# Loads ahead of the gate setup, eight output buffers, a short last slot and an earlier first unit in a block-sorted attention feeding a mixture of experts

## The chip, the core and the metric

The kernel runs on one core of a Trainium2 chip. The metric is the device time of one execution in microseconds (us). The core has a matrix engine (TensorE: PE in the profile, its weight loads PEld), a vector engine (VectorE, DVE), an activation engine (ScalarE, ACT), a general engine (GpSimd, POOL) and a sync engine (SyncE, SP). Each works off its own instructions in program order; they meet through semaphores. POOL and SP also issue the DMAs: POOL all bulk loads and all indirect scatters, SP the small loads and the transposing reads.

## What is computed

```python
# attention: batch 4, heads 8, seq 768, head_dim 64, 8 blocks of 96
P = sort_net                                  # (4, 8, 8, 8)
for _ in range(5):                            # Sinkhorn
    P = exp(P - max(P, -1)); P = P / sum(P, -1); P = P / sum(P, -2)
k_sorted = einsum('bhij,bhjcd->bhicd', P, k_blocks)
v_sorted = einsum('bhij,bhjcd->bhicd', P, v_blocks)
attn = softmax(q_blocks @ k_sorted.T / 8) @ v_sorted    # per block
x = attn as (3072 tokens, 512)
# mixture of experts: 8 experts, one per token, F = 1024
logits = x @ w_gate + modality_bias[modality_id]
e = argmax(logits); gate = softmax(logits)[e]
out[token] = gate * (relu(x[token] @ w1[e]) @ w2[e])
```

In the inputs drawn here two experts take all tokens, one 1559 rows and the other 1513.

## The kernel before

**Stages.** The two halves of the batch are groups g = 0 and 1. For each group `sort_k` multiplies the k blocks with the Sinkhorn matrix, `sort_v` does so for v (64 matmuls of 128 columns in all per group). Then the attention runs in 32 units u = 0 to 31 (16 a group): `scores(u)` writes PSUM, `expo(u)` takes the exponential on ACT, `av(u)` multiplies with v and normalises on DVE into `xb`. `spread_q` (called by `prep_s`, a DVE copy) and `prep_q` (PE transposes and one evacuation) make the queries of a unit. `scores(1)` stands behind `prep_q(2)` in PE's order, and that needs the spread made by `prep_s(2)`.

**Routing.** Eight units make a quarter m (0 to 3) of the tokens. `gate_T`/`gate_L` (lines 395 to 413) form the logits in four steps, `choose(m)` takes the argmax on DVE, `place(m)` (line 437) ranks the tokens on PE (`rk`, line 444) and scatters the rows to DRAM (`xs_scratch`) by eight indirect DMAs on POOL (line 472), sorted by expert. `table(m)` computes on DVE which slots of 256 rows are now full.

**Experts.** 13 slots of up to 256 rows. Slots 0 to 11 alternate between the two experts, slot 12 takes the leftover of one. A slot is fetched by `x_fetch` (transposing DMA on SP, line 584, plus a small one for row numbers and gates, line 587) and worked off in six pieces: four `mL1(s, j)` (8 matmuls of 256 columns each into `hp`, then a relu on DVE or ACT) and two `mL2(s, t)` (8 matmuls of 512 columns into `yp`, gate product into one of four `y` buffers, indirect DMA to `out`, line 638). Slot 12 reads its weights at an address from a register.

**Order.** `tc.manual_schedule()`: program order is each engine's order. The main loop over u issues `scores(u)`, `expo(u)`, the work listed in `A1[u]`, `p1` pieces, `av(u-1)`, `prep_q(u+2)`, `prep_s(u+3)`, the work listed in `A2[u]`, `p2` pieces. `pace(u)` gives p1 and p2. The sort of group 1 is spread over units 6 to 15 by `A2`. Which of ACT and DVE evacuates a PSUM tile is decided by `pick` when the program is built.

**Around the change.** Behind the sort of group 0 stand, in this order, `prep_q(0)`, `prep_q(1)`, a mask and an iota on POOL, `gate_consts()` (line 265: `perm_mult` multiplies on POOL into `ptmpw`, line 191, and reduces on DVE into `wgf`, line 192; then six small POOL operations), and only then the loads of k, v, weights (expert 0) and the first half of the queries for group 1. In POOL's order they come behind `gate_consts`. `load_w(1)` and the second half of the queries, `load_q(1, 1)`, are issued in `A2[9]`, right behind `place(0)`.

Of the kernel before, what the change touches and what calls it, by code (L numbers as in the profile page):

```python
# [17 lines left out]
def kernel(  # L18
# [28 lines left out]
    NS = 13  # L47
# [23 lines left out]
    k_raw = kvb[:, RW:2 * RW]  # L71
    v_cols = kvb[:, 0:128 * D].rearrange("p (c d) -> p d c", d=D)
# [7 lines left out]
    xTg = [singles.tile([128, 8, BLK], BF16, tag=f"xTg{z}", name=f"xTg{z}") for z in range(2)]  # L80
    y_b = [singles.tile([128, Dm], FP32, tag=f"y{z}", name=f"y{z}") for z in range(4)]
    xT_b = [singles.tile([128, 4, PR], BF16, tag=f"xT{z}", name=f"xT{z}") for z in range(3)]
    idg_b = [singles.tile([128, 2, 2], I32, tag=f"idg{z}", name=f"idg{z}") for z in range(4)]
    hT_b = [qTb[0][:, 2048 + z * 2048:4096 + z * 2048].rearrange("p (f r) -> p f r", f=8) for z in range(2)]
    zpad = singles.tile([128, GW], BF16, tag="zpad")
# [29 lines left out]
    def load_q(g, hh):  # L115
        t = q_in(g, hh).rearrange("p (r h f) -> p r h f", r=2, h=4)
        for par in range(2):
            nc.gpsimd.dma_start(out=t[:, par], in_=q[2 * g + par, 4 * hh:4 * hh + 4]
                                .rearrange("h (p t) d -> p h (t d)", t=6))

# [65 lines left out]
    def perm_mult(dst, srcs, nm):  # L186
        eng = nc.gpsimd if nm == "w" else nc.vector
        tmp = small.tile([128, 4, E, E], FP32, tag=f"ptmp{nm}", name=f"ptmp{nm}")
# [304 lines left out]
    def table(m):  # L493
# [29 lines left out]
        if last:  # L523
            mk, t1 = t_("mk", 2), t_("t1", 1)
            nc.vector.tensor_tensor(a, f[:, 0:2], d2, ALU.subtract)
            nc.vector.tensor_scalar(mk, a, 0.0, None, ALU.is_gt)
            nc.vector.tensor_tensor(t1, mk[:, 0:1], mk[:, 1:2], ALU.mult)
# [53 lines left out]

    def x_fetch(s, row, own, after=()):
        view = xs_dram[bass.ds(row, PR)]
        i1 = nc.sync.dma_start_transpose(out=xT_b[s % 3], in_=view.bitcast(BF16)[:, 0:Dm])
        if own:
            nc.sync.nop()
        i2 = nc.sync.dma_start(out=idg_b[s % 4], in_=pair_rows(row)[:, :, Dm // 2:GW // 2])
        if own:
            for i in (i1, i2):
                in_xs_group(i.ins, after)  # L590
                for a in after:
                    tc.add_manual_dep(i.ins, a.name, SYNC, reason="rows of the slot")

    def x_load(s, after=()):
# [5 lines left out]
        row = nc.values_load(tb[0:1, n:n + 1], engines=(SPEng,), min_val=0, max_val=ZR)  # L600
        x_fetch(s, row, True, after)

    evs = {}

    def mE(s):
        evs[s] = nc.values_load(tabL[0:1, 1:2], engines=(PEng,), min_val=0, max_val=WCOL)

    def w_at(s, off, n):
        if s in evs:
            return w01[:, bass.ds(evs[s] + off, n)]  # L610
        return w01[:, (s % 2) * WCOL + off:(s % 2) * WCOL + off + n]

    def mL1(s, j):
        hp = mipsum.tile([128, 2, PR], FP32, tag="mi", name=f"hp{s}_{j}")
        for f in range(2):
            for c in range(4):
                nc.tensor.matmul(hp[:, f], w_at(s, c * F + (2 * j + f) * 128, 128), xT_b[s % 3][:, c],  # L617
                                 start=(c == 0), stop=(c == 3))
        hd = hT_b[s % 2][:, 2 * j:2 * j + 2]
        if not pick(0.61, 0.7):  # L620
            nc.vector.tensor_scalar(hd, hp, 0.0, None, ALU.max)  # L621
        else:
            nc.scalar.activation(hd, hp, ACT.Relu)  # L623

    def mL2(s, t):
        yp = mipsum.tile([128, Dm], FP32, tag="mi", name=f"yp{s}_{t}")
        for fc in range(8):
            nc.tensor.matmul(yp, hT_b[s % 2][:, fc, t * 128:(t + 1) * 128],  # L628
                             w_at(s, 4 * F + fc * Dm, Dm), start=(fc == 0), stop=(fc == 7))
        idg = idg_b[s % 4]  # L630
        y = y_b[(2 * s + t) % 4]
        gate = idg.bitcast(FP32)[:, t, 1:2]
        if pick(0.7, 0.7):
            nc.scalar.activation(y, yp, ACT.Copy, scale=gate)  # L634
        else:
            nc.vector.tensor_scalar(y, yp, gate, None, ALU.mult)  # L636
# [5 lines left out]
        tc.add_to_no_dep_group("out", ins.ins)  # L642

# [5 lines left out]
    def late_consts():  # L649
# [28 lines left out]
    nc.gpsimd.iota(zpad.bitcast(I32)[:, Dm // 2:Dm // 2 + 1], pattern=[[0, 1]], base=SKIP, channel_multiplier=0)  # L678
# [62 lines left out]
    def run_pieces(n):
        for _ in range(n):
            if st["pos"] >= len(pieces):
                return
            for f, a in pieces[st["pos"]]:
                f(*a)
                if f is mL1 and a[1] == 3:
                    st["l1"] = a[0] + 1
                if f is mL2 and a[1] == 1:
                    st["done"] = a[0] + 1  # L750
                if f is not mE:
                    x_try()
            st["pos"] += 1

    def pace(u):
        if u < 16:
            return 0, 0
        if u < 22:
            return 1, 1
        if u < 24:  # L760
            return 0, 0
        if u < 30:
            return 1, 1
        return 1, 1

    prep_s(2)
    for u in range(32):
        p1, p2 = pace(u)
        scores(u)
        expo(u)  # L770
        for f, a in A1.get(u, []):
# [15 lines left out]
    choose(3)  # L787
    run_pieces(1)
    place(3)
# [35 lines left out]
    nc.vector.tensor_tensor(tR2, rv, sF256[:, 0:NREST], ALU.add)  # L825
    evs.clear()
    for s in range(NREST):
# [40 lines left out]
```

## Time and profile before

| | us |
|---|---|
| median of 3 runs | 257.69 (254.66 to 259.04) |
| the profiled execution | 253.83 |
| its span, first to last instruction | 252.1 |
| PE busy in it | 176.5 (70%) |
| DVE / ACT / POOL busy in it | 102.7 / 93.5 / 73.8 |

All rows of the trace belong to the profiled execution: times are us from the start of its span. In a timeline row stand start, duration, engine, line, operation, output tile <- input tiles, shapes, count, and in brackets the idle time of the engine before it with what ended it. PEclk is the granted clock of TensorE as a share of its full 2.4 GHz; 0.5 is 1.2 GHz.

### The profile page before, as it was taken

The numbers are of one execution on the slowest core, as the hardware profiler recorded it, in microseconds if no ns is written. First come the engines' busy times: TensorE is split into PE (matmuls) and PEld (weight loads), VectorE is DVE, ScalarE is ACT, GpSimd is POOL, SyncE is SP. The second block draws the span as 40 slices with busy tenths as digits, with TensorE's granted clock in tenths as the row PEclk, the third lists the DMA queues.
The fourth block names the chain that finished last, engine by engine and source line by source line (L and its number), as shares of the span: only waits on it lengthen the run. The fifth ranks groups of instructions, "written<-read, shape, count | busy, mean of one in ns | idle before, by whom it ended". The sixth has DMA issues, their size and how long they took to land.

```text
span 252.1 us, 5223 instructions
## 1 busy us (share of the span) xinstructions
PE 176.5 (70%) x2046; PEld 126.8 (50%) x2046; DVE 102.7 (41%) x340; ACT 93.5 (37%) x146; POOL 73.8 (29%) x101
## 2 busy tenths in 40 slices
PE   0079689785880968189869249998808999999800
PEld 0079578674770735065654136665603666665300
DVE  6858775862660561045463013435401233322200
ACT  2148667555580423154432224433203322232200
POOL 7201380035610027401106700322761223333110
PEclk9999965957586779569797858999986999999965
DMA  5999779999799902531102365231545343322000
GB/s 88 218 201 193 105 134 217 200 189 203 165 192 188 154 13 83 135 64 42 44 3 62 101 131 43 84 86 43 163 106 130 106 125 104 111 83 78 4 15 0
DMA packets 33840, 27.78 MB, mean 110 GB/s; under 512 B 22543, under 2 KB 29455, under 8 KB 33552
## 3 DMA queue, kind: packets, MB, share of 16 engines
q0 software_dynamic: 11840, 23.10, 41.7%
q1 hardware_dynamic: 21968, 4.28, 12.1%
q8 instruction: 18, 0.29, 0.5%
q14 instruction: 14, 0.11, 0.1%
HBM read 27.33 MB, written 10.78 MB: 151 GB/s over the span
## 4 chain that ended last, share of the span: by engine, by line
PE 21%; issue 19%; DMA 9%; POOL 8%; another core or an unknown queue 5%; DVE 4%; ACT 2%; POOLq 1%; DVEq 0%; ACTq 0%
PE yp L628 8%; DMA q_in<-in_q_dram 7%; PE hp L617 7%; POOL out_dram L638 6%; POOL xs_scratch L472 2%; PE sc L366 1%; DMA xs_scratch<-xb,dest 1%; PE lg L404 1%; PE gt L398 1%; DVE xb L389 1%; PE op L385 1%; ACT xTg L295 1%; ACT attnT L372 1%; POOLq L638 1%
## 5 line engine op out<-in xcount | busy, mean ns | idle before, releaser
L617 PE MATMUL hp<-xT,w 128*128 128x256 bf16 x416 | 57.8, 290 | 6.7 <-DMA xT<-xs_scratch 6.7
L628 PE MATMUL yp<-w,qT 128*128 128x512 bf16 (+1 forms) x208 | 52.8, 407 | 7.9 <-ACT qT L623 7.9
L617 PEld LDWEIGHTS <-w 128*128 128x128 bf16 (+1 forms) x416 | 41.4, 103 | 17.4 <-issue 7.3
L472 POOL DMA_INDIRECT xs_scratch<-xb,dest x32 | 29.4, 917 | 67.0 <-issue 63.2
L638 POOL DMA_INDIRECT out_dram<-y,idg x26 | 25.4, 976 | 77.1 <-ACT y L634 53.6
L628 PEld LDWEIGHTS <-qT 128*128 128x128 bf16 x208 | 20.7, 103 | 32.1 <-ACT qT L623 9.4
L623 ACT ACTIVATE qT<-hp 128x512 bf16<-128x512 f32 x33 | 19.6, 596 | 44.5 <-PE hp L617 33.5
L372 ACT ACTIVATE attnT<-sc 96x768 bf16<-96x768 f32 x32 | 25.8, 808 | 17.0 <-remote 9.4
L621 DVE TENSOR_SCALAR qT<-hp 128x512 bf16<-128x512 f32 x19 | 13.1, 692 | 44.8 <-PE hp L617 34.4
L634 ACT ACTIVATE y<-yp,idg 128x512 f32<-128x512 f32 x18 | 12.4, 687 | 35.9 <-PE yp L628 25.6
L389 DVE TENSOR_TENSOR xb<-op,rs 96x512 bf16<-96x512 f32 x32 | 22.0, 687 | 1.4 <-DMA q_in<-in_q_dram 0.2
L404 PE MATMUL lg<-wgp,xTg 128*96 128x8 bf16 x128 | 9.9, 201 | 17.7 <-ACT xTg L295 15.4
L388 DVE RECIPROCAL rs<-op 96x8 f32<-96x8 f32 x32 | 6.4, 199 | 35.4 <-PE op L385 20.3
L404 PEld LDWEIGHTS <-xTg 128*96 128x96 bf16 x128 | 8.9, 151 | 19.1 <-ACT xTg L295 15.9
L636 DVE TENSOR_SCALAR y<-yp,idg 128x512 f32<-128x512 f32 x8 | 6.0, 751 | 29.7 <-PE yp L628 27.0
L385 PE MATMUL op<-v_sb,attnT 96*128 96x65 bf16 x256 | 15.8, 211 | 0.2 <-issue 0.2
L295 ACT CAST v_sb<-va 96x512 bf16<-96x512 f32 (+1 forms) x23 | 13.3, 641 | 5.8 <-PE va L317 4.6
L385 PEld LDWEIGHTS <-attnT 96*128 96x128 bf16 x256 | 13.5, 110 | 3.2 <-issue 0.6
L308 PEld LDWEIGHTS <-kvb 128*64 128x64 bf16 x384 | 9.8, 145 | 9.5 <-issue 9.3
L295 ACT COPY qT<-tq 128x768 bf16<-128x768 bf16 x12 | 9.6, 799 | 12.4 <-PE tq L350 12.4
L366 PE MATMUL sc<-qT,kT 64*128 64x96 bf16 (+1 forms) x256 | 13.1, 232 | 1.5 <-ACT attnT L372 1.2
L317 PE MATMUL va<-bd,kvb 128*128 128x128 bf16 x128 | 13.7, 275 | 0.0
(155 smaller groups left out, 171.2 us busy)
## 6 DMA issues: line engine op xcount, KB each, us to landing
w<-in_moe_w_dram POOLq DMA_DIRECT2D x4, 1024.0 KB
kvb<-in_k_dram POOLq DMA_DIRECT2D x4, 768.0 KB
kvb<-in_v_dram POOLq DMA_DIRECT2D x2, 1536.0 KB
v_sb<-in_q_dram POOLq DMA_DIRECT2D x4, 384.0 KB
q_in<-in_q_dram POOLq DMA_DIRECT2D x4, 384.0 KB
xs_scratch<-zpad SPq DMA_DIRECT2D x3, 258.0 KB
xs_scratch<-xb,dest POOLq DMA_INDIRECT x32
out_dram<-y,idg POOLq DMA_INDIRECT x26
```

Of the source, the lines that this page charges most:

```text
L295: (nc.scalar.copy if pick(act, dve) else nc.vector.tensor_copy)(dst, src)
L317: nc.tensor.matmul(acc[:, z], v_cols[:, d0 + z], bd[g], start=True, stop=True)
L366: nc.tensor.matmul(sc[0:m, par, j * BLK:(j + 1) * BLK], kT[g][rows, x0:x0 + m], qT[rows, i], start=True, stop=True)
L372: nc.scalar.activation(attnT[u % 2][:, 0:8 * BLK].rearrange("p (r f) -> p r f", r=2), sc_tiles.pop(u)[0:BLK, :, 0:4 * BLK], ACT.Exp, scale ...
L385: nc.tensor.matmul(ov[:, par, j], attnT[u % 2][:, c0:c0 + 128], v_sb[g][0:BLK, par * 64 + h * 8 + i, 0:D + 1], start=True, stop=True)
L389: nc.vector.tensor_tensor(xt[:, :, h * D:(h + 1) * D].rearrange("p (r j) d -> p r j d", r=2), ov[0:BLK, :, :, 0:D], rs.broadcast_to([BLK, ...
L404: nc.tensor.matmul(lg[:, t], xTg[c % 2][:, t], wgp[:, c], start=True, stop=True)
L472: ins = nc.gpsimd.indirect_dma_start(out=xs_dram, out_offset=bass.IndirectOffsetOnAxis(ap=dest[:, t:t + 1], axis=0), in_=xt.bitcast(I32)[: ...
L617: nc.tensor.matmul(hp[:, f], w_at(s, c * F + (2 * j + f) * 128, 128), xT_b[s % 3][:, c], start=(c == 0), stop=(c == 3))
L623: nc.scalar.activation(hd, hp, ACT.Relu)
L628: nc.tensor.matmul(yp, hT_b[s % 2][:, fc, t * 128:(t + 1) * 128], w_at(s, 4 * F + fc * Dm, Dm), start=(fc == 0), stop=(fc == 7))
L638: ins = nc.gpsimd.indirect_dma_start(out=out, out_offset=bass.IndirectOffsetOnAxis(ap=idg[:, t, 0:1], axis=0), in_=y, in_offset=None, boun ...
```

## The change

1. k of group 1 gets a place of its own in `kvb` (a gap of 2048 columns is put in and zeroed by DVE at the start), and its two loads are issued after the k sort of group 0. The loads of v, of the first half of the queries and of the weights of expert 0 come before `gate_consts`, which now stands between `scores(0)`/`expo(0)` and `prep_q(1)`.
2. `prep_s(0)`, `prep_q(0)`, `scores(0)` and `expo(0)` are called inside the v sort (after jobs 13 and 16 of 21).
3. `load_q(1, 1)` and `load_w(1)` move from `A2[9]` to `A1[10]` and wait until the transposing read of slot 0 has landed.
4. `place(1)` and `place(2)` move one step later, behind the next unit's `scores`; `table_x` follows them. Two pieces instead of one between `choose(3)` and `place(3)`.
5. Eight `y` buffers in `kvb`, four `xT` and six `idg` buffers, `hT` 0 in a tile of its own.
6. From slot 6 on the `mL1` of the next slot are mixed with the `mL2` of the current one. Pieces run from u = 17 on, two a unit, without the pause at 22 and 23 (30 pieces in the loop instead of 28).
7. Slot 12 takes up to 128 rows: rows stationary, 512 columns of w1 moving (`last_L1`), eight transposes (`last_T`), one `last_L2`, the gate product split between ACT and DVE.

```diff
-    kvb = singles.tile([128, 2 * RW], BF16, tag="kvb")
+    KO = 128 * D
+    kvb = singles.tile([128, KO + RW], BF16, tag="kvb")
...
+    NY, NX, NI = 8, 4, 6
+    yo = [KO + z * 2 * Dm for z in range(6)] + [RW + z * 2 * Dm for z in range(2)]
+    y_b = [kvb[:, o:o + 2 * Dm].bitcast(FP32) for o in yo]
...
+    nc.vector.memset(kvb[:, RW:KO], 0.0)
...
+    def last_L1(n):
+        if n == 0:
+            lreg["w"] = nc.values_load(tabL[0:1, 1:2], engines=(PEng,), min_val=0, max_val=WCOL)
+        hp = mipsum.tile([128, 512], FP32, tag="mi", name=f"hl{n}")
+        for c in range(4):
+            nc.tensor.matmul(hp, xT_b[SL % NX][:, c, 0:128], wl_at(c * F + n * 512, 512),
+                             start=(c == 0), stop=(c == 3))
+        relu(hrow[n], hp)
+    def last_T():
...
+        for f in range(8):
+            nc.tensor.transpose(tp[:, f], hrow[f // 4][:, (f % 4) * 128:(f % 4 + 1) * 128], ident)
...
+    def last_L2():
...
+        for fc in range(8):
+            nc.tensor.matmul(yp, hT_b[SL % 2][:, fc, 0:128], wl_at(4 * F + fc * Dm, Dm),
+                             start=(fc == 0), stop=(fc == 7))
...
+    make_upper_triangular(nc, maskUT, val=1.0, diag=False)
...
     for n, (f, g, x0, kd) in enumerate(g0):
         f(g, x0, kd)
...
             late_consts()
-        if n == 17:
+            load_k(1, 0)
+            load_k(1, 1)
+        if n == 13:
             prep_s(0)
-    prep_q(0)
+        if n == 16:
+            prep_q(0)
+            scores(0)
+            expo(0)
+    load_v(1)
+    load_q(1, 0)
+    load_w(0)
+    gate_consts()
     prep_q(1)
-    make_upper_triangular(nc, maskUT, val=1.0, diag=False)
...
-    gate_consts()
-    load_k(1, 0)
-    load_k(1, 1)
-    load_v(1)
-    load_w(0)
-    load_q(1, 0)
     zero_block()
...
+    def late_loads():
+        first = load_q(1, 1)
+        tc.add_manual_dep(first.ins, xins[0].ins.name, SYNC, reason="rows of the first slot go ahead")
+        load_w(1)
...
-            at2(8 * m + 9, place, m)
-            at1(8 * m + 10, table_x, m)
-    at2(9, load_w, 1)
-    at2(9, load_q, 1, 1)
+            at2(8 * m + 9, place, m) if m == 0 else at1(8 * m + 10, place, m)
+            at1(8 * m + 10, table_x, m) if m == 0 else at2(8 * m + 10, table_x, m)
+    at1(10, late_loads)
...
+        nx = l1s(s + 1) if PIPE <= s + 1 <= SL else []
+        h = len(nx) // 2
+        pieces += nx[:h] + [(mL2, (s, 0))] + nx[h:] + ([(last_T, ())] if s == SL - 1 else []) + [(mL2, (s, 1))]
+    pieces.append((last_L2, ()))
...
     def pace(u):
...
+        return (1, 1) if u >= 17 else (0, 0)
...
     choose(3)
-    run_pieces(1)
+    run_pieces(2)
     place(3)
```

## Rows read from the trace of the kernel before

**Rows 1.** The timeline of PE in the expert tail; sixteen or 32 matmuls a row

```profile
198.25 3.62 PE L628 MATMUL yp<-w,qT 128*128 128x512 bf16 x16
...
229.49 5.65 PE L617 MATMUL hp<-xT,w 128*128 128x256 bf16 x32
234.99 3.61 PE L628 MATMUL yp<-w,qT 128*128 x16
```

**Rows 2.** Windows: stretch, length, busy PE, PEld, DVE, ACT, POOL, PEclk, DMA share, GB/s

```profile
139.90:148.20 8.30, 0.06 (x2) 0.03 (x1) 0.66 (x2) 1.69 (x3) 3.96 (x5) 0.66 0.49 131
```

**Rows 3.** The timeline of POOL: scatters of `place(0)` and of `place(1)`

```profile
54.07 1.02 POOL L472 DMA_INDIRECT xs_scratch<-xb,dest  x1 [16.70 <-issue]
...
61.42 0.91 POOL L472 DMA_INDIRECT xs_scratch<-xb,dest  x1 [1.45 <-DMA w<-in_moe_w_dram]
...
92.66 0.98 POOL L472 DMA_INDIRECT xs_scratch<-xb,dest  x1 [22.45 <-issue]
...
101.26 0.90 POOL L472 DMA_INDIRECT xs_scratch<-xb,dest  x1 [0.30 <-issue]
...
103.78 0.98 POOL L638 DMA_INDIRECT out_dram<-y,idg  x1 [0.30 <-issue]
```

**Rows 4.** The timeline of PE: two long waits ahead of the first expert slots

```profile
60.59 0.73 PE L404 MATMUL lg<-wgp,xTg 128*96 128x8 bf16 x8 [3.07 <-ACT xTg L295]
...
81.30 1.87 PE L617 MATMUL hp<-xT,w 128*128 128x256 bf16 x8 [6.68 <-DMA xT<-xs_scratch]
```

**Rows 5.** The waits of the whole span: us in total, times, longest

```profile
POOL out_dram L638 <- ACT y L634: 53.6, 12, 12.7
...
PE rk L444 <- DVE oh L430: 7.4, 4, 2.5
```

**Rows 6.** The timeline of SP: transposing reads of slots 0 and 2

```profile
68.39 1.81 SPq L584 DMA_TRANSPOSE xT<-xs_scratch  x1
...
103.69 1.34 SPq L584 DMA_TRANSPOSE xT<-xs_scratch  x1
```

**Rows 7.** The timeline of PE at the start of the units

```profile
19.96 6.07 PE L317 MATMUL va<-bd,kvb 128*128 128x128 bf16 x64
...
27.73 0.35 PE L366 MATMUL sc<-qT,kT 64*128 64x96 bf16 x8 [0.31 <-DVE qT L295]
28.80 0.51 PE L350 MATMUL tq<-ident,q_il 128*128 128x128 bf16 x6 [0.72 <-DVE q_il L125]
```

**Rows 8.** The timeline of DVE at the start of the kernel and of the units

```profile
1.81 0.27 DVE L157 MEMSET zpad<- 128x258 uint32 x1
...
23.91 2.34 DVE L295 CAST v_sb<-va 96x1024 bf16<-96x1024 f32 x2
26.18 0.61 DVE L125 COPY q_il<-v_sb 128x768 bf16<-128x768 bf16 x2
...
28.06 0.41 DVE L192 TENSOR_REDUCE wgf<-ptmpw 128x32 f32<-128x256 f32 x1
```

**Rows 9.** The timeline of POOL: gate setup and the loads of group 1

```profile
21.16 1.01 POOL L191 TENSOR_TENSOR ptmpw<-wg_sb,perm 128x256 f32<-128x256 f32 x1 [13.18 <-DVE perm L257]
...
33.03 0.55 POOL L113 DMA_DIRECT2D kvb<-in_v_dram  x1
34.02 0.76 POOL L575 DMA_DIRECT2D w<-in_moe_w_dram  x1 [0.45 <-issue]
34.77 0.91 POOL L577 DMA_DIRECT2D w<-in_moe_w_dram  x1
35.65 1.52 POOL L118 DMA_DIRECT2D q_in<-in_q_dram  x2
```

**Rows 10.** Windows as in the second group: two stretches of the first units

```profile
34.00:44.00 10.00, 9.99 (x171) 8.90 (x168) 6.43 (x16) 6.81 (x10) 3.35 (x5) 0.52 1.03 210
44.00:51.00 7.00, 4.62 (x152) 3.98 (x152) 5.68 (x17) 3.54 (x7) 0.00 (x0) 0.96 1.00 200
```

**Rows 11.** The costliest groups: busy us, mean ns; the relu on ACT

```profile
L623 ACT ACTIVATE qT<-hp 128x512 bf16<-128x512 f32 x33 | 19.6, 596 | 44.5 <-PE hp L617 33.5
```

More of the change, by code (lines that the diff above doesn't have):

```diff
@@ L68 @@
     w01 = singles.tile([128, 2 * WCOL], BF16, tag="w01")
[L69 removed]
+    KO = 128 * D
+    kvb = singles.tile([128, KO + RW], BF16, tag="kvb")
     v_in = kvb[:, 0:RW]
[L71 removed]
+    k_raw = kvb[:, KO:KO + RW]
     v_cols = kvb[:, 0:128 * D].rearrange("p (c d) -> p d c", d=D)
@@ L116, in load_q @@
         t = q_in(g, hh).rearrange("p (r h f) -> p r h f", r=2, h=4)
-        for par in range(2):
-            nc.gpsimd.dma_start(out=t[:, par], in_=q[2 * g + par, 4 * hh:4 * hh + 4]
-                                .rearrange("h (p t) d -> p h (t d)", t=6))
+        return [nc.gpsimd.dma_start(out=t[:, par], in_=q[2 * g + par, 4 * hh:4 * hh + 4]
+                                    .rearrange("h (p t) d -> p h (t d)", t=6)) for par in range(2)][0]
     def spread_q(g, hq):
@@ L580, in stage_of, with x_fetch @@
         return 0 if s < 2 else 1 if s < 4 else 2 if s < 8 else 3
-    def x_fetch(s, row, own, after=()):
-        view = xs_dram[bass.ds(row, PR)]
-        i1 = nc.sync.dma_start_transpose(out=xT_b[s % 3], in_=view.bitcast(BF16)[:, 0:Dm])
+    xins = {}
+    def x_fetch(s, row, own, after=(), n=PR):
+        view = xs_dram[bass.ds(row, n)]
+        i1 = nc.sync.dma_start_transpose(out=xT_b[s % NX][:, :, 0:n], in_=view.bitcast(BF16)[:, 0:Dm])
+        xins[s] = i1
         if own:
             nc.sync.nop()
-        i2 = nc.sync.dma_start(out=idg_b[s % 4], in_=pair_rows(row)[:, :, Dm // 2:GW // 2])
+        i2 = nc.sync.dma_start(out=idg_b[s % NI], in_=pair_rows(row)[:, :, Dm // 2:GW // 2])
         if own:
@@ L600, in x_load, with relu @@
         row = nc.values_load(tb[0:1, n:n + 1], engines=(SPEng,), min_val=0, max_val=ZR)
[L601 to L606, printed above, removed]
+        x_fetch(s, row, True, after, 128 if s == NS - 1 else PR)
     def w_at(s, off, n):
-        if s in evs:
-            return w01[:, bass.ds(evs[s] + off, n)]
         return w01[:, (s % 2) * WCOL + off:(s % 2) * WCOL + off + n]
+    def relu(dst, src):
+        if not pick(0.61, 0.7):
+            nc.vector.tensor_scalar(dst, src, 0.0, None, ALU.max)
+        else:
+            nc.scalar.activation(dst, src, ACT.Relu)
     def mL1(s, j):
@@ L616, in mL1, with y_out @@
             for c in range(4):
-                nc.tensor.matmul(hp[:, f], w_at(s, c * F + (2 * j + f) * 128, 128), xT_b[s % 3][:, c],
+                nc.tensor.matmul(hp[:, f], w_at(s, c * F + (2 * j + f) * 128, 128), xT_b[s % NX][:, c],
                                  start=(c == 0), stop=(c == 3))
[L619 to L631, printed above, removed]
-        gate = idg.bitcast(FP32)[:, t, 1:2]
[L633 to L636, printed above, removed]
+        relu(hT_b[s % 2][:, 2 * j:2 * j + 2], hp)
+    def y_out(s, t, n, parts):
+        idg = idg_b[s % NI]
+        gate = idg.bitcast(FP32)[:, t, 1:2]
+        y = y_b[n % NY]
+        for z, (eng, dst, src) in enumerate(parts(y)):
+            if eng:
+                nc.scalar.activation(dst, src, ACT.Copy, scale=gate)
+            else:
+                nc.vector.tensor_scalar(dst, src, gate, None, ALU.mult)
         nc.gpsimd.nop()
@@ L642, in mL2, with wl_at @@
         tc.add_to_no_dep_group("out", ins.ins)
+    def mL2(s, t):
+        yp = mipsum.tile([128, Dm], FP32, tag="mi", name=f"yp{s}_{t}")
+        for fc in range(8):
+            nc.tensor.matmul(yp, hT_b[s % 2][:, fc, t * 128:(t + 1) * 128],
+                             w_at(s, 4 * F + fc * Dm, Dm), start=(fc == 0), stop=(fc == 7))
+        y_out(s, t, 2 * s + t, lambda y: [(pick(0.7, 0.7), y, yp)])
+    SL = NS - 1
+    hrow = [xTg[z].rearrange("p a b -> p (a b)")[:, 0:512] for z in range(2)]
+    lreg = {}
+    def wl_at(off, n):
+        return w01[:, bass.ds(lreg["w"] + off, n)]
+    def last_L1(n):
[7 more added lines that the diff above has]
+    def last_T():
+        tp = mipsum.tile([128, 8, 128], BF16, tag="mi", name="htl")
+        for f in range(8):
+            nc.tensor.transpose(tp[:, f], hrow[f // 4][:, (f % 4) * 128:(f % 4 + 1) * 128], ident)
+        nc.scalar.copy(hT_b[SL % 2][:, 0:4, 0:128], tp[:, 0:4])
+        nc.vector.tensor_copy(hT_b[SL % 2][:, 4:8, 0:128], tp[:, 4:8])
+    def last_L2():
+        yp = mipsum.tile([128, Dm], FP32, tag="mi", name="ypl")
+        for fc in range(8):
+            nc.tensor.matmul(yp, hT_b[SL % 2][:, fc, 0:128], wl_at(4 * F + fc * Dm, Dm),
+                             start=(fc == 0), stop=(fc == 7))
+        h = Dm // 2
+        y_out(SL, 0, 2 * SL, lambda y: [(True, y[:, 0:h], yp[:, 0:h]), (False, y[:, h:], yp[:, h:])])
     from concourse.masks import make_upper_triangular
@@ L744, in run_pieces @@
                 return
[L745 to L752, printed above, removed]
+            f, a = pieces[st["pos"]]
+            f(*a)
+            if f is mL1 and a[1] == 3:
+                st["l1"] = a[0] + 1
+            if f is mL2 and a[1] == 1:
+                st["done"] = a[0] + 1
+            x_try()
             st["pos"] += 1
     def pace(u):
[L756 to L764, printed above, removed]
+        return (1, 1) if u >= 17 else (0, 0)
     prep_s(2)
@@ L768 @@
         p1, p2 = pace(u)
-        scores(u)
-        expo(u)
+        if u:
+            scores(u)
+            expo(u)
         for f, a in A1.get(u, []):
```

37 lines of the change are left out of this document (19 added, 18 removed).

## The prediction

> **What bounds the kernel now.** I read the page first: PE is the busiest engine, but 70% of the span leaves 76 us in which it does nothing, so the question is where these lie. The timelines of PE, DVE and POOL answer it, then the waits, then windows over the stretches that stand out.
>
> At the start PE follows the landing of k and v and the Sinkhorn chain on DVE. From 19.96 it sorts v, at 27.73 comes `scores(0)`, at 28.80 `prep_q(2)` [rows 7]. Then it is PE that limits: from 34 to 44 it is busy 9.99 of 10 us at a granted clock of 0.52, the lower level of 1.2 GHz for nearly all of it; from 44 to 51 it is busy 4.62 of 7 us at 0.96 [rows 10].
>
> Later there are waits of four kinds. Behind each burst of eight scatters of `place` comes a stretch in which nothing computes: in 139.90 to 148.20 PE works 0.06 us, DVE and ACT little, and POOL only issues [rows 2]. The scatters stand 1.2 us apart (92.66 to 101.26 for the eight of `place(1)`), and two of `out` follow at once [rows 3]. In `place(0)` the stretch is short, 3.07 us [rows 4], because its scatters are spread out by landing transfers (61.42 waits 1.45 us for w [rows 3]). PE waits 6.68 us at 81.30 for the rows of slot 0 [rows 4], whose transposing read was issued at 68.39 [rows 6]: 12.9 us from issue to use, with the weights of expert 1 and half the queries queued ahead of it. It waits four times, 7.4 us together, for `choose` on DVE ahead of the rank matmul [rows 5]. From 198.25 to 238.60 PE goes from piece to piece, and slot 12 costs 9.1 us there, 229.49 to 238.60 [rows 1]; 13.5 us follow to the end of the span, with gate product, scatter and landing.
>
> **The change, part by part.** The sum is made against the profiled execution, 253.83 us. The median of the three runs, 257.69, is 1.015 times that; I multiply at the end.
>
> *Start: +7.4.* The gap in `kvb` is cleared on DVE ahead of the Sinkhorn chain: 2048 columns of bf16 are 1024 words, and 258 words took 0.27 us [rows 8], so 1.07 us; some 0.1 hides behind input landings, 0.95 stays. v's sort begins at 20.9. `prep_s(0)`, `prep_q(0)` and `scores(0)` stand inside it, but they need DVE for a cast (1.17, half of the row of two) and a spread (0.61) [rows 8], then a transposition and its evacuation, some 0.5 each: `scores(0)` comes at about 27.7, where it was [rows 7]. So the early unit gains nothing by itself. Some 20 of the 64 matmuls of the sort still stand behind it in PE's order, 6.07 x 20/64 = 1.9 [rows 7]: the sort ends at 30.0 and not at 26.03.
>
> This end matters because `load_v(1)` writes over the v that the sort reads. It now stands on POOL ahead of `gate_consts`, so POOL waits for it, and then issues v (0.55), q (1.52), w (0.45 idle, 0.76, 0.91), then computes `ptmpw` (1.01) [rows 9]: 5.2 us, until 35.2. On DVE the reduction into `wgf` (0.41 [rows 8]) is waiting for that, and DVE is in order: behind it stand the spread for units 2 and 3 (0.61) and all normalising of unit 0. PE's next instruction of weight, `prep_q(2)`, needs this spread: 35.2 + 0.41 + 0.61 = 36.2 where it was 28.80. Late by 7.4; then PE is the limit again, so it is not caught up. Lower bound: the sort ends at 26.03 as before and the clear is hidden, 26.03 + 5.2 + 0.41 + 0.61 + 0.2 for the hops = 32.4, +3.6. Upper: another 1.6 if each of the four gaps on POOL takes the 0.45 seen once [rows 9], +9. The k loads moved ahead of all this sit in a time in which POOL was idle for 13.18 us [rows 9]: nothing.
>
> By the rows this idle time of PE costs no clock where it falls: the units behind it run at 0.52 already [rows 10]. The Trainium skill, "TensorE: Matmul & The Clock Gate", Part 1 (The HAM clock gate), says that a PE that has been idle drops to 1.2 GHz and gets 2.4 GHz back by activity; by that rule the new idle time could hand the lower level on to the units behind, and the sum would be 2.2 us more; no row here shows it.
>
> *Slot 0: -6.7.* w(1) and the second half of the queries now wait for the transposing read. Without them ahead of it I take 2.4 to 4.2 us for it, plus its issue of 1.81 [rows 6]; with the eighth scatter at about 70 it lands at 77. The first piece is now in unit 17, not 16, some 2 us behind 81.30. The wait of 6.68 goes (bounds -6.68 and -3, if a piece fewer in unit 16 leaves PE idle elsewhere). Against it: the queries of later units now land at about 84, and are wanted at 86 to 90; w(1) at about 97, wanted in unit 20, not before 97. This is close; it is the last rival below.
>
> *Rank waits: -4.0.* At m = 1, 2 and 3 a piece (1.9 us in [rows 4]) or `scores` now stands between `choose` and `rk`. The waits of 7.4 have a longest of 2.5 [rows 5]; the one of `place(0)` stays, the other three shrink by some 1.3 each. Bounds -5 and 0.
>
> *Slot 12: -4.3.* Before: 9.1. Now 16 matmuls of 512 columns, 3.62/16 = 0.226 each [rows 1], 3.6; eight transposes at 0.08 make 0.6; one relu that is not covered, 0.6 [rows 11]: 4.8. Bounds -5 (transposes covered) and -3 (weights addressed by a register are slower: before, 32 matmuls of 256 columns took 5.65 [rows 1], 0.18 each where 3.62/32 would be 0.11).
>
> *Bursts: +0.6.* In `place(0)` the loads of w and q that held its scatters back are issued without k ahead of them and have landed; the burst is then as tight as that of `place(1)`, and its dead stretch goes from 3.07 [rows 4] towards 8.3 [rows 2]: +4.2 (5.2 less 1 for what lands in it anyway). In `place(1)` and `place(2)` fewer scatters of `out` are joined to the eight (two in [rows 3]): one or two times 1.2 each, -3.6. Unknown in size: bounds -5 and +5.
>
> *Nothing:* eight `y` buffers. The one large wait on them is POOL's for y (53.6 us in 12 [rows 5]), and that is the scatter waiting for the product, which more buffers don't shorten; in the tail PE has no gap for them to close [rows 1], and the same holds for mixing `mL1` with `mL2`. More `xT` and `idg` buffers bring reads forward whose data isn't there earlier. One DVE operation more in the last table, 0.15. The cover for all these is PE's own work; without it they cost under 1 us.
>
> Sum: 253.8 + 7.4 - 6.7 - 4.0 - 4.3 + 0.6 = 246.8, times 1.015 = 250.5.
>
> **Rivals.**
>
> *The start costs little* (0.15). PE was idle for 2.4 us between 44 and 51 [rows 10]; with k there earlier, that may take up part of the delay, and with the lower bound of 3.6 the start costs 1.2: 240.6, or 244. For it: the k sort of group 1 can fill any unit once k has landed. Against it: the stretch ahead, 34 to 44, has no idle time at all.
>
> *The bursts give the gain back* (0.20). If the stretch behind a burst is set by the scatters alone, an earlier `rk` only brings its begin forward: the 4.0 of the rank waits come back as dead time, 250.8, or 254.6. For it: the stretches are all near 8 us although different work stands ahead of them. Against it: PE's work between `choose` and `rk` is work that is not left for later.
>
> *The lower clock is handed on* (0.10). If 44 to 51 too runs at 1.2 GHz after the new idle time, its 4.62 us of PE become 4.62 x 0.96/0.5 = 8.9, 1.9 more than the 7 of the stretch, and I add 0.3 for its idle time that isn't filled: +2.2, so 249.0, or 252.7. For it: 34 to 44 is at 0.52 behind a start of short bursts. This is the case of the page named above. Against it: the stretch reached 0.96 after ten busy us, and these still stand ahead of it.
>
> *Slower: the hold on the late loads* (0.12). If the read of slot 0 takes its 12.9 us [rows 4, 6] for another reason than the loads ahead of it (the scatters still in flight), then q(1,1) is issued only at 87, lands at 94 and w(1) at 104: 8 us late for the queries, 7 more at worst for w(1), 255 to 262, or 259 to 266. It decides from a landing of slot 0 behind about 79. Against it: two large loads do stand ahead of it in the queues now.
>
> **How the numbers follow.** The forecast (0.43) has its own range from 246 to 254. What three runs of this kernel can tell from no change is about 2%, 5 us, so faster means below 252.5. Of the forecast some 0.06 lies above that; the cheap start (0.15) lies below; half the clock case (0.05) too: faster 0.57. The bursts (0.20), the other half of the clock and the 0.06 make same 0.31; the hold makes slower 0.12. The range 241 to 260 leaves out most of the hold and the low end of the cheap start.
>
> **What would show it.** On DVE an idle time of some 7 us ahead of `wgf`, ended by `ptmpw`, and `prep_q(2)` near 36. No wait of PE for xT ahead of the first expert slot; POOL waiting for xT ahead of `load_q(1, 1)`, not beyond 79. Waits of `rk` of 3 to 4 us in all. A slot 12 of 4.8 us. A dead stretch of 7 us or more behind `place(0)`. A clock near 1 in the units before `place(0)`. The prediction is wrong if `wgf` does not wait (then 243), or if the spreads of units 20 on, or slot 1, wait for late loads.

## The result and the profile after

| | before | after |
|---|---|---|
| median of 4 runs, us | 257.84 (254.66 to 259.04) | 246.41 (245.85 to 247.75) |
| ratio | | 0.960, 95% interval 0.951 to 0.970 |
| span of the profiled execution, us | 252.1 | 243.9 |
| PE busy / not busy in it, us | 176.5 / 75.6 | 170.2 / 73.7 |

The changed kernel is 4.0% faster. One thing has to be said ahead of all else: the experiments ran on four chips, each group of runs with its own runs of the kernel before, and on three of the four the kernel before took 223 to 226 us and not 256 to 258. On the one of the three on which the changed kernel ran as it is, it is slower. Ratios to the kernel before on the same chip are therefore what is compared below; a ratio of one chip beside a ratio of another is less sure than two from the same chip, and the text says where it does that. Some executions are over 1.5% slower than the fastest of the same kernel; ratios and intervals leave these out, among them two of the kernel before at 328 and 335 us.

PE's busy time in this trace is a little too small: of 2022 matmuls 11 have no record, as the counts of PE and of its weight loads on the page show.

```profile
PE 170.2 (70%) x2011; PEld 124.3 (51%) x2022; DVE 103.6 (42%) x344; ACT 91.9 (38%) x145; POOL 72.5 (30%) x100
```

The start. Timelines of the changed kernel (start, duration, engine, line, operation, in brackets the idle time before it and what ended it), POOL, DVE and PE in turn:

```profile
18.41 0.59 POOL L114 DMA_DIRECT2D kvb<-in_k_dram  x1 [10.34 <-PE ka L312]
...
30.49 0.53 POOL L117 DMA_DIRECT2D kvb<-in_v_dram  x1 [9.33 <-PE va L321]
...
34.48 0.75 POOL L195 TENSOR_TENSOR ptmpw<-wg_sb,perm 128x256 f32<-128x256 f32 x1
...
46.49 0.20 POOL L273 CAST modF<-modI 96x32 f32<-96x32 int32 x1 [10.46 <-DMA modI<-in_moe_modality_id_dram]
...
35.27 0.42 DVE L196 TENSOR_REDUCE wgf<-ptmpw 128x32 f32<-128x256 f32 x1 [4.18 <-POOL ptmpw L195]
...
49.01 0.22 DVE L414 TENSOR_TENSOR lacc<-lg,biasm 96x64 f32<-96x64 f32 x1 [5.47 <-POOL biasm L282]
...
36.02 0.82 PE L354 MATMUL tq<-ident,q_il 128*128 128x128 bf16 x6 [5.18 <-DVE q_il L128]
...
50.13 0.82 PE L402 MATMUL gt<-ident,xb 96*128 96x96 bf16 x8 [4.84 <-DVE xb L393]
```

`load_v(1)` waits on POOL for the sort of v to end, `ptmpw` comes behind the loads, DVE waits for it, and `prep_q(2)` starts at 36.02 where it was 28.80 [rows 7]. Then a second wait, which was not there before: POOL waits 10.46 us for the modality ids, `biasm` is made from them, DVE's first sum of logits needs `biasm`, and behind it in DVE's order is the normalising of `xb` on which PE waits 4.84.

The windows that answer to [rows 10] (stretch, length, busy PE, PEld, DVE, ACT, POOL, PEclk, DMA share, GB/s), and below them those behind the four `place`, which answer to [rows 2]:

```profile
34.00:44.00 10.00, 7.90 (x104) 6.56 (x105) 5.55 (x15) 4.84 (x7) 1.51 (x3) 0.50 1.14 208
44.00:51.00 7.00, 2.16 (x31) 1.76 (x29) 1.03 (x4) 2.08 (x3) 2.46 (x6) 0.50 1.23 222
...
67.00:77.00 10.00, 3.43 (x53) 2.75 (x50) 1.81 (x10) 2.80 (x5) 7.41 (x8) 0.50 0.26 73
100.00:110.00 10.00, 5.52 (x63) 3.97 (x63) 2.00 (x11) 3.60 (x5) 7.37 (x8) 0.84 0.26 72
138.00:150.00 12.00, 6.16 (x68) 3.93 (x67) 2.92 (x13) 3.03 (x5) 7.28 (x8) 0.98 0.28 85
175.00:190.00 15.00, 7.47 (x54) 5.06 (x53) 3.50 (x26) 2.77 (x5) 9.21 (x10) 0.90 0.44 134
```

The kernel before, the same kind of row for `place(1)` and `place(3)`:

```profile
99.90:107.80 7.90, 1.05 (x9) 0.42 (x5) 0.78 (x2) 2.21 (x4) 3.80 (x4) 0.61 0.56 138
...
181.60:189.70 8.10, 0.21 (x1) 0.00 (x0) 0.00 (x0) 0.60 (x1) 4.70 (x5) 0.83 0.45 121
```

PE's idle time behind the four bursts was 3.1, 6.9, 8.2 and 7.9 us, and is 6.6, 4.5, 5.8 and 7.5: 26.1 and 24.4 in all. The windows are not of one length, 27.4 us together before and 47.0 after, so that the 24.4 can hold idle time that is not of the bursts; the difference is a rough one.

The waits of PE and POOL in the changed kernel (total, times, longest), which answer to [rows 5]:

```profile
POOL q_in L121 <- DMA xT<-xs_scratch: 5.7, 1, 5.7
...
PE rk L448 <- DVE oh L434: 3.6, 3, 1.7
```

And the end of the tail, which answers to [rows 1]:

```profile
222.31 1.03 PE L663 MATMUL hl<-w,xT 128*128 x4
...
224.90 1.03 PE L663 MATMUL hl<-w,xT 128*128 x4
225.76 0.39 PE L670 MATMUL htl<-ident,xTg 128*128 128x128 bf16 x4
226.61 0.40 PE L670 MATMUL htl<-ident,xTg 128*128 128x128 bf16 x4 [0.47 <-issue]
...
228.57 1.89 PE L677 MATMUL ypl<-w,hT 128*128 x8
```

Slot 12, now of up to 128 rows, takes 0.86 + 0.86 (to the next instruction), 0.39 + 0.40 with 0.47 of waiting, and 1.89: 4.9 us for 9.1. No wait of PE for xT is left in this trace.

### The profile page after: what moved, and what is told of

It reads as the page before. It is cut to its first block, busy times and chain, and to the rows that moved or that the text cites. A ratio compares the mean times of both kernels' runs of the same rounds, so it can differ in the third digit from the quotient of the medians.

```text
span 243.9 us, 5078 instructions
## 1 busy us (share of the span) xinstructions
PE 170.2 (70%) x2011; PEld 124.3 (51%) x2022; DVE 103.6 (42%) x344; ACT 91.9 (38%) x145; POOL 72.5 (30%) x100
## 4 chain that ended last, share of the span: by engine, by line
PE 49%; issue 9%; another core or an unknown queue 8%; DVE 4%; ACT 3%; DMA 1%; POOL 0%; POOLq 0%; DVEq 0%; ACTq 0%
PE hp L624 18%; PE yp L647 17%; PE va L321 2%; PE gt L402 2%; PE lg L408 2%; PE op L389 2%; PE sc L370 2%; PE tq L354 1%; DMA xs_scratch<-xb,dest 1%; DVE xb L393 1%; ACT qT L618 1%; PE ypl L677 1%; PE hl L663 1%; ACT xTg L299 1%
## 5 line engine op out<-in xcount | busy, mean ns | idle before, releaser
L638 POOL DMA_INDIRECT out_dram<-kvb,idg x25 | 24.4, 976 | 72.1 <-ACT kvb L634 30.4
L624 PEld LDWEIGHTS <-w 128*128 128x128 bf16 x384 | 37.0, 101 | 15.5 <-issue 7.8
L647 PE MATMUL yp<-w,qT 128*128 128x512 bf16 x91 | 25.1, 407 | 4.8 <-ACT qT L618 2.6
L647 PE MATMUL yp<-w,hT 128*128 128x512 bf16 x90 | 24.7, 414 | 0.3
L618 ACT ACTIVATE qT<-hp 128x512 bf16<-128x512 f32 x16 | 9.4, 597 | 25.2 <-remote 13.3
L634 ACT ACTIVATE kvb<-yp,idg 128x512 f32<-128x512 f32 x13 | 8.9, 686 | 24.0 <-PE yp L647 18.4
L647 PEld LDWEIGHTS <-qT 128*128 128x128 bf16 x96 | 9.3, 102 | 15.0 <-issue 4.4
L618 ACT ACTIVATE hT<-hp 128x512 bf16<-128x512 f32 x18 | 10.6, 594 | 15.5 <-PE hp L624 15.3
L408 PEld LDWEIGHTS <-xTg 128*96 128x96 bf16 x128 | 8.6, 146 | 14.5 <-ACT xTg L299 11.4
L354 PE MATMUL tq<-ident,q_il 128*128 128x128 bf16 x96 | 11.0, 271 | 6.9 <-DVE q_il L128 6.8
L647 PEld LDWEIGHTS <-hT 128*128 128x128 bf16 x96 | 9.7, 105 | 10.4 <-issue 2.9
(172 smaller groups left out, 219.7 us busy)
```

The lines of the kernel that those rows point to most:

```text
L354: nc.tensor.transpose(tp[:, t], src[:, t], ident)
L408: nc.tensor.matmul(lg[:, t], xTg[c % 2][:, t], wgp[:, c], start=True, stop=True)
L618: nc.scalar.activation(dst, src, ACT.Relu)
L638: ins = nc.gpsimd.indirect_dma_start(out=out, out_offset=bass.IndirectOffsetOnAxis(ap=idg[:, t, 0:1], axis=0), in_=y, in_offset=None, boun ...
```

## The experiments

### The two kernels where nothing stands still

Both kernels unchanged, on one other chip. (A standstill is here a stretch behind a burst of scatters in which the engines all but stop. In the kernel before there are three of some 8 us and one of 3.1, and not four of 8 as the first expectation has it.)

> The changed kernel as it is, on the chip of the following runs. In the first experiments the kernel before took 224 us and nothing stopped behind its scatters; where it took 258 us, four stretches of some 8 us stood still. Theory: the start costs the changed kernel its 12 us on either chip (wgf and the modality ids), and what it saves elsewhere is partly time of the standstill; where nothing stands still it takes 236 to 242 us, slower than the kernel before. Rival: its savings are the same on both, and it stays 4% ahead, at about 215.

> The kernel before as it is, for its profile on the same chip. Theory: the standstill behind the scatters is a property of the chip or of the hour and not of the program: on a chip where it takes 224 us the gaps of 8 us are gone, and PE waits only for xT ahead of the first slots; on one where it takes 258 us they are there.

Measured: before 225.63, after 232.36, ratio 1.036 (1.027 to 1.046): slower, as the theory has it, though less than its 236 to 242. The line of busy times on the page, for the kernel before and for the changed one there:

```profile
PE 165.4 (75%) x2046; PEld 121.3 (55%) x2046; DVE 102.9 (47%) x340; ACT 93.1 (42%) x146; POOL 74.1 (34%) x101
```

```profile
PE 167.3 (73%) x2022; PEld 124.1 (54%) x2022; DVE 103.3 (45%) x344; ACT 91.5 (40%) x145; POOL 72.6 (32%) x100
```

Their spans are 221.0 and 229.3. In the kernel before the stretches behind `place(1)` to `place(3)` are full of work:

```profile
97.50:105.50 8.00, 8.00 (x114) 6.19 (x113) 4.36 (x10) 6.31 (x9) 5.87 (x8) 1.00 0.28 79
126.00:134.00 8.00, 7.48 (x102) 5.56 (x101) 2.75 (x8) 5.03 (x8) 5.92 (x7) 1.00 0.31 97
160.00:168.00 8.00, 8.00 (x56) 5.30 (x55) 1.97 (x3) 2.72 (x5) 6.03 (x7) 1.00 0.40 116
```

So the standstill does not come from the program alone: the same program has it in one group of runs and not in another. Each chip was met in one group only, so that chip and hour can't be told apart; below, "a chip with standstills" is short for such a group. Between the two groups the kernel before differs by 31.1 us of span, 20.0 in idle time of PE (75.6 against 55.6) and 11.1 in PE's busy time (176.5 against 165.4), and the changed kernel by 14.6 (11.7 and 2.9, less exact for the 11 records). That the changed kernel loses less because it waits there anyway fits the traces, but was not tested. Its two longest waits of PE on this chip, beyond the start:

```profile
141.26 1.87 PE L624 MATMUL hp<-xT,w 128*128 128x256 bf16 x8 [6.41 <-DMA xT<-xs_scratch]
178.32 2.10 PE L624 MATMUL hp<-xT,w 128*128 128x256 bf16 x9 [5.30 <-DMA xT<-xs_scratch]
```

Slots 4 and 8 wait for the rows of `place(2)` and `place(3)`: without the pause in units 22 and 23 and with `place(2)` later, the pieces run out of rows (an argument; the pause was not put back by itself on this chip). On the first chip neither wait shows. The kernel before has one long wait of this kind, for slot 0:

```profile
81.88 0.37 PE L617 MATMUL hp<-xT,w 128*128 128x256 bf16 x1 [11.06 <-DMA xT<-xs_scratch]
```

By these rows, the change on this chip: start +7.1 (28.63 to 35.76), ids +4.8, slot 0 -11.1, slots 4 and 8 +11.7, slot 12 -4.2, rank waits -1.4 (7.2 to 5.8): +6.9 of the 8.3 found in the spans.

### The order at the start

Three kernels on one chip with 224.2 us before. Gate setup first:

```diff
+    gate_consts()
     load_v(1)
     load_q(1, 0)
     load_w(0)
-    gate_consts()
```

> One part of the changed kernel undone: the gate setup stands ahead of the loads of v, queries and weights again (the k loads stay early). Theory: two waits at the start come from this order, the reduction into wgf waiting for ptmpw behind the loads (DVE 4.18 us, PE 5.18 us) and the logits waiting for the modality ids (DVE 5.47 us, PE 4.84 us), whose 4-byte packets share the engines with the bulk loads. Then prep_q(2) comes at about 32 and not at 36.0, the ids land in the low 30s, and the time falls by 7 to 9 us from 246.4 to about 238. Rival: the k loads alone, which are still ahead, hold the ids, the loads queue behind the ids on POOL, and the time is 244 to 249.

Measured 223.4 (219.7 to 225.1) against 224.2 before, a ratio of about 0.996 for which there is no interval, where the unchanged version stands at 1.036 on another chip: some 4%, 9 us, as the theory has it. `prep_q(2)` comes at 31.93 with a short wait, and the ids are waited for until 36.48, later than expected but with nothing on DVE behind them:

```profile
31.93 0.82 PE L354 MATMUL tq<-ident,q_il 128*128 128x128 bf16 x6 [0.91 <-DVE q_il L128]
```

The k loads late (`load_k(1, 0)`, `load_k(1, 1)` behind `gate_consts()`):

> The changed kernel with the two k loads of group 1 moved behind the gate setup; nothing else. Theory: without k in flight the ids land at about 30, as before the change (29.4), the logits do not wait, and the time falls by the 4.8 us of PE's wait, to about 242; wgf waits as it did and prep_q(2) stays at 36. Rival: v, queries and weights, issued at 30 to 34, are enough to hold the ids, or k lands too late for its sort in unit 5: 245 or more.

Measured 236.7, ratio 1.054 (1.041 to 1.067): the rival. The ids cost nothing now, but the k sort of group 1 waits for k. (The changed kernel also begins this sort in unit 5 and not in unit 6, which the list of the change leaves out.) POOL and PE of this run:

```profile
35.99 0.30 POOL L273 CAST modF<-modI 96x32 f32<-96x32 int32 x1
...
59.40 1.50 PE L312 MATMUL ka<-bd,kvb 128*64 128x64 bf16 x48 [11.95 <-DMA kvb<-in_k_dram]
```

Both together, the order of the kernel before:

```diff
+    gate_consts()
+    load_k(1, 0)
+    load_k(1, 1)
     load_v(1)
-    load_q(1, 0)
     load_w(0)
-    gate_consts()
+    load_q(1, 0)
```

> The changed kernel with part 1 undone whole: gate setup, then k, v, weights, queries, in the order of the kernel before. Theory: both waits of the start go, prep_q(2) at 32, ids at about 30, 238 us or a little less than with the gate setup first and k early. Rival: early bulk loads are worth something, k and v land late for the sort of group 1, and PE waits for them between 45 and 60: 243 or more.

Measured 226.6, ratio 1.009 (1.003 to 1.016). The same POOL row in the version with gate setup first and k early, and in this one:

```profile
36.48 0.21 POOL L273 CAST modF<-modI 96x32 f32<-96x32 int32 x1 [4.54 <-DMA modI<-in_moe_modality_id_dram]
```

```profile
31.95 0.30 POOL L273 CAST modF<-modI 96x32 f32<-96x32 int32 x1
```

With no bulk load ahead the ids are there by 31.95, with k ahead at 36.48, with k, v, queries and weights ahead at 46.49. In the run with k late they are there by 35.99, but there they had all but landed before v, queries and weights went out: of the packets under 512 bytes 1897 start between 24 and 28 us, 171 in the twelve us behind.

How the loads hold the ids up stands in the trace of DMA packets. The bulk loads are on queue q0, the ids on SP's queue q1. Two stretches of the changed kernel on the first chip, 24 to 28 us (k on the way) and 28 to 40 us (then v too); queue, kind, packets, MB, share of 16 engines:

```profile
q0 software_dynamic: 893, 0.83, 125.2%
q1 hardware_dynamic: 892, 0.00, 30.0%
```

```profile
q0 software_dynamic: 365, 2.61, 104.0%
q1 hardware_dynamic: 365, 0.00, 4.2%
```

The two queues go packet for packet. The 3072 ids are packets of 4 bytes each, and they advance by one for each bulk packet: when q0's packets are large (2.61 MB in 365), 365 in 12 us. In the kernel before, where q0 runs out of work in this time, q1 has 1938 packets between 24 and 28 against 820 on q0.

Putting the gate setup behind the loads is what costs 9 us. What loading k early is worth stays open. The 223.4 and 226.6 have no interval between them and their runs overlap (219.7 to 225.1, 223.7 to 227.3), and in the slower version PE has no wait for k or v: DVE waits 4.9 us for the second half of the queries, where it waits 0.7 in the faster one, and the rank waits are 8.5 and not 4.3.

### The hold on the late loads

```diff
-        tc.add_manual_dep(first.ins, xins[0].ins.name, SYNC, ...)
...
-    at1(10, late_loads)
+    at2(9, load_w, 1)
+    at2(9, load_q, 1, 1)
```

> The changed kernel with part 3 undone: the second half of the queries and w(1) are issued right behind the scatters of place(0), without waiting for the read of slot 0. Theory of the prediction: the hold removes a wait of 6.7 us, so without it PE waits for xT again and the time is about 253. Rival: the read is issued at 78.6 and first used at 93.4, so even 12.9 us from issue to use fit; the wait is gone because the first piece comes later, and the time stays at 246 within 1.5 us.

Measured 241.0, ratio 1.077 (1.066 to 1.087) against 1.036 on another chip: some 9 us worse, the theory of the prediction. The wait for slot 0 is 5.9 of them; where the other 3 lie wasn't traced. SP's read of slot 0 and PE's first use of it:

```profile
78.21 1.71 SPq L591 DMA_TRANSPOSE xT<-xs_scratch  x1
...
92.68 1.87 PE L624 MATMUL hp<-xT,w 128*128 128x256 bf16 x8 [5.93 <-DMA xT<-xs_scratch]
```

14.5 us from issue to use with the loads beside it; with the hold, on the first chip, the read issued at 78.59 had landed by 82.36, when POOL went on.

### The later place

```diff
-            at2(8 * m + 9, place, m) if m == 0 else at1(8 * m + 10, place, m)
-            at1(8 * m + 10, table_x, m) if m == 0 else at2(8 * m + 10, table_x, m)
+            at2(8 * m + 9, place, m)
+            at1(8 * m + 10, table_x, m)
...
-    run_pieces(2)
+    run_pieces(1)
     place(3)
```

> The changed kernel with place(1) and place(2) back at their old place, right behind choose, and one piece between choose(3) and place(3). Theory of the prediction: PE waits 4 us more for the three rank matmuls and the time grows by that. Rival: rows reach their slots earlier, PE waits less for xT of slots 2 and 4, and the time stays the same or falls by 1 to 3 us.

Measured 233.3, ratio 1.038 (1.026 to 1.049), the same as the changed kernel. Its waits, and then those of the changed kernel on this chip:

```profile
PE rk L448 <- DVE oh L434: 10.3, 4, 5.5
PE hp L624 <- DMA xT<-xs_scratch: 9.4, 2, 4.8
```

```profile
PE hp L624 <- DMA xT<-xs_scratch: 11.7, 2, 6.4
...
PE rk L448 <- DVE oh L434: 5.8, 3, 3.7
```

The rank waits grow by 4.5 as the theory wants, the waits for xT shrink by 2.3 as the rival wants. The time is the rival's: the same.

### Buffers and mixing

`NY, NX, NI = 4, 3, 4` and `PIPE = 12` (mixing for slot 12 alone), and then `PIPE = 12` alone:

> The changed kernel with four y buffers, three xT and four idg buffers, and mL1 and mL2 not mixed but for the last slot. Theory of the prediction: these edits cost and save nothing, same as the changed kernel within 1 us. Rival: scatters of out hold buffers during the bursts of place, products wait for them, and the tail grows by 3 us or more.

> The changed kernel with eight y buffers, four xT and six idg buffers as it has them, but mL1 and mL2 not mixed except for the last slot. The version with few buffers and without mixing took 227.0 us against 232.4. Theory: mixing put mL1(8), which waits for xT of slot 8, ahead of an mL2 that could run; without it about 229 to 230, the rest of the 5 us belonging to the buffers. Rival A: all 5 us belong to the mixing, 227. Rival B: all belong to the buffers, 232.

The first: 227.0, ratio 1.012 (1.002 to 1.022), 5.3 us better than the changed kernel beside it; neither expectation. Its waits:

```profile
PE hp L624 <- DMA xT<-xs_scratch: 10.2, 2, 6.7
...
PE rk L448 <- DVE oh L434: 3.6, 3, 1.6
```

The wait for xT is 1.5 shorter, the rank waits 2.2 shorter. The second ran on a chip with standstills (255.6 before): 243.9, ratio 0.958 (0.948 to 0.967), the same as the changed kernel's 0.960 on the first chip. As no wait for slot 8 shows where there are standstills, this run doesn't tell mixing from buffers: which of them costs the 5 us stays open.

### Pieces held back, and the gate setup first

```diff
-        return (1, 1) if u >= 17 else (0, 0)
+        return (0, 0) if u < 17 else (1, 0) if 20 <= u < 24 else (1, 1)
```

> The changed kernel with the four pieces held back alone. Theory: PE's waits for xT ahead of slots 4 and 8 come from pieces that run sooner than place(2) and place(3) deliver; without them 222 to 225 where the changed kernel takes 232. On a chip with standstills these waits fall into the standstill and the gain is under 4 us. Rival: the waits only move into units 20 to 23: 230 to 233.

> The changed kernel with two things undone: the gate setup ahead of the loads of v, queries and weights, and four expert pieces held back (in units 20 to 23 one piece a unit and not two; 26 pieces in the loop). Theory: the two waits of the start (12 us together) and PE's two waits for xT of slots 4 and 8 (6.4 and 5.3 us) are separate and add up. On a chip on which nothing stands still behind the scatters: 232 - 9 - 10 = 212 to 215, 5% below the kernel before. Rival: the held pieces leave PE idle in units 20 to 23 by as much as they save later, 222 to 225.

Both on the chip with 255.6 us before. Held pieces alone: 246.7, ratio 0.964 (0.952 to 0.976), no change against the 0.960 of the first chip, as the theory has it for such a chip. With the gate setup first as well: 237.2, ratio 0.931 (0.921 to 0.941), 4% better than the version with held pieces alone, 3% better than the changed kernel on the first chip, and the best on this kind of chip. The two differ in the order at the start alone, which is thus worth 9.5 us here (both on one chip) and some 9 on the other kind (across two chips). Whether holding the pieces back gains 10 us where nothing stands still, as both expectations have it, this chip couldn't show.

The last run adds two multiplications on POOL between the scatters of `place(0)` and `place(1)`:

```diff
+            if t and m < 2:
+                for _ in range(2):
+                    nc.gpsimd.tensor_tensor(gapt, gapt, gapt, ALU.mult)
```

> The version with the gate setup first and four pieces held back, and in place(0) and place(1) two small multiplications on POOL between the scatters, so that they stand some 1.9 us apart and not 1.21. In the kernel before, PE stood still while place(0)'s scatters came 1.21 apart and went on while the last three came 1.9 to 2.3 apart. Theory: the standstill needs scatters at the close distance; where it occurs (a kernel before of some 256 us) it is gone behind place(0) and place(1), no gap of PE there over 2 us, and the ratio to the kernel before falls from 0.931 to about 0.915. Rival: each scatter has its standstill, or the rows come later and PE waits for xT: 0.93 or more. On a chip without standstills (224 us before) the spacing does nothing and the run tells whether the two waits of the start and the two for xT add up: 211 to 216, ratio 0.945 to 0.965; if not, 220 or more.

It met a chip without standstills: 217.6 against 223.3, ratio 0.977 (0.972 to 0.982), between the two expectations for such a chip (211 to 216, 220 or more); what spacing does to a standstill wasn't tested. The scatters stand some 2.1 us apart. The waits for xT are nearly gone, but there is another one, on DVE and then on PE:

```profile
PE rk L450 <- DVE oh L434: 9.6, 3, 6.7
...
DVE q_il L128 <- DMA q_in<-in_q_dram: 5.1, 1, 5.1
...
PE hp L629 <- DMA xT<-xs_scratch: 3.1, 3, 2.0
```

The spacing delays the read of slot 0 (the eight scatters take 16.0 us from first to last, against 9.6 in the version with the gate setup first), the queries are held until it has landed, a spread on DVE waits 5.1 us for them, and `choose(1)` stands behind that spread. Less these 5.1 us it would be 212.5, in the range expected. That is an estimate which puts the whole wait down to the spacing; DVE waits 0.7 us here with the gate setup first alone, and the version with the pieces held back and no spacing didn't run on such a chip. So whether the gains add up isn't shown. It is the fastest version that ran on that kind of chip, and both kernels are beaten on either kind by a version with the gate setup first and the pieces held back, where nothing stands still with the spacing too.

## Why the prediction was right, and where it wasn't

| step, us | forecast | measured on the first chip |
|---|---|---|
| start, `prep_q(2)` 28.80 to 36.02 | +7.4 | +7.2 |
| ids | none | +4.8 |
| slot 0 | -6.7 | -6.7 |
| rank waits, 7.4 to 3.6 | -4.0 | -3.8 |
| slot 12, 9.1 to 4.9 | -4.3 | -4.2 |
| bursts, 26.1 to 24.4 | +0.6 | -1.7 |
| pause in units 22 and 23 | 0 | not taken apart |
| sum | -7.0 | -4.4 of the -8.2 in the span |

**Start.** Right to 0.2 us, with the mechanism as told: the sort's end, POOL's five instructions, DVE in order behind `wgf`. The bounds of 3.6 to 9 were not needed; the rival of a cheap start falls. (The upper bound adds 1.6 for four gaps of 0.45 on POOL; these make 1.8, or 1.35 without the one that is in the 5.2 already. Nothing rests on it.)

**Ids, the step that failed.** The prediction has the k loads moved ahead "in a time in which POOL was idle", at a price of nothing, and the wait for the ids in no term at all. It asked what an issue costs its queue, not what the transfer does to other transfers. The six small loads of ids are on the way until 29.4 in the kernel before; with the 5888 KB of k, v, queries and weights beside them they last until 46.49, and the runs on the order show the steps between. The row for it was at hand: `modF` is the first instruction behind `wgp` in the setup that was moved, and its row in the kernel before has a wait of 0.60 us on the same DMA:

```profile
29.40 0.20 POOL L269 CAST modF<-modI 96x32 f32<-96x32 int32 x1 [0.60 <-DMA modI<-in_moe_modality_id_dram]
```

The Trainium skill, "DMA: Bandwidth & Descriptors", Queues, rings and completion order, says that each DMA engine goes round the queues it has work for, packet by packet. The trace agrees: 893 packets on one queue and 892 on the other, then 365 and 365.

**The lower clock.** The rival of [rows 10] came true in its sign: 44 to 51 runs at 0.50, the lower level, where it had 0.96, with 2.16 us of PE work in it and not 4.62. By "TensorE: Matmul & The Clock Gate", Part 1 (The HAM clock gate), of the Trainium skill a PE that idles is put at 1.2 GHz; the trace agrees, 0.50 behind the idle 5.18 us. But the 4.84 us wait for the ids is in the same stretch, so that its price isn't told apart from it here. The 0.96 was no fixed property of the kernel before either: on the chip without standstills it has 0.60 there:

```profile
44.00:51.00 7.00, 6.50 (x152) 5.77 (x152) 4.57 (x11) 3.77 (x6) 0.00 (x0) 0.60 0.98 197
```

A sign that the prediction named failed: the clock in the units before `place(0)` was not near 1, but 0.65 from 51 to 60 us and 0.79 from 60 to 67.

**Slot 0.** Right, and shown by undoing the hold: the wait is back with 5.9 us, and the time is some 9 longer. The rival against it, that the hold itself makes queries late, was right too where other time is gone: on the chips without standstills DVE waits 2.1 us for them in the changed kernel and 5.1 us in the last experiment. The bound, that it decides from a landing "behind about 79", was wrong: on the first chip the read landed by 82.36 and nothing waited, because the units had become later by 12 us too.

**Rank waits.** Right in the row and wrong in what it is worth: -3.8 in the trace, yet undoing it on a chip without standstills changes the time by 0.9 of 232 us, as rows that come sooner shorten the waits for xT by 2.3.

**Slot 12** was right to 0.1 us: 16 matmuls 3.6, transposes 0.8, the step that is not covered 0.5. **Buffers and mixing** were costed at nothing; on a chip without standstills they cost 5.3 us together, and which of the two isn't settled. **Bursts** were taken as a fixed cost of the program. They aren't, and with them goes the sign of the result: 0.960 on the chip with standstills, 1.036 on the one without. Behind `place(0)` the stretch grew, 3.1 to 6.6, as told and not quite to the 7 named as a sign.

**The rest of the sum, and luck.** Of the -8.2, 3.8 us are in none of the rows. Filling the pause in units 22 and 23 may be in there (PE's idle time between 120 and 130 fell from 2.3 to 0.05 us), but it was not measured by itself. PE's busy time fell by 6.3, 2.1 more than slot 12 explains, but the 11 missing records are worth as much as that (2.4 us at 0.22 each), so nothing follows from it. So the time came out right in part by luck: the ids cost 4.8 us that the sum didn't have, and the bursts (2.3 less than forecast) and these 3.8 gave 6.1 that it didn't have either. It was luck too that the result was measured on a chip with standstills.

## What to carry to other kernels

When a bulk load is moved forward, list every small transfer still on the way and the first instruction that waits for it: here 4-byte ids came 17 us later, and PE waited 4.8 us for them. A setup step that many things need goes ahead of loads that wait for a buffer on the same queue, even if the loads are large. And if an engine's pieces run faster than rows arrive, the gain turns into waits for rows; that it pays to hold work back for that long is not shown: by itself it gained nothing on the chip with standstills, and on the other kind it ran only together with other edits.

## What was not expected of the hardware

In two of the five groups of runs a burst of eight scatters 1.2 us apart nearly stops all engines; in the others it doesn't show, and for the kernel before as it is that rests on one trace. POOL issues at the same distance in both, and the DMA engines are about half idle in the stretches behind `place(1)` to `place(3)` (share 0.45 to 0.56 in the windows of the kernel before; behind `place(0)`, where loads are on the way, it is 1.26). PE of the changed kernel on the first chip, in the burst of `place(2)`:

```profile
143.98 0.39 PE L647 MATMUL yp<-w,qT 128*128 128x512 bf16 x1
145.43 0.59 PE L647 MATMUL yp<-w,qT 128*128 128x512 bf16 x2 [1.06 <-issue]
146.65 0.38 PE L647 MATMUL yp<-w,qT 128*128 128x512 bf16 x1 [0.62 <-issue]
147.37 0.38 PE L647 MATMUL yp<-w,qT 128*128 128x512 bf16 x1 [0.35 <-issue]
```

These matmuls wait for nothing that the profile shows ("issue") and come 0.72 us apart at the end, where others of this kind take 0.22. In this burst it goes on until 149.5, 2 us behind the end of the last scatter. What makes one chip, or one hour, do this and another not, and whether wider spacing avoids it, is open: the one run for it met a chip on which it doesn't occur.
